# Attention scores as float32 products of two heads on the two row halves of the array, instead of float32r parts of one head

## The chip, the core and the metric

The kernel runs on one core of a Trainium2 chip. The metric is device time in microseconds of one execution; the median of three runs is given. The core has five engines with queues of their own: PE (TensorE, matmuls; PEld is its weight load), DVE (VectorE), ACT (ScalarE), POOL (GpSimd) and SP, which here issues the DMAs. Each engine takes its instructions in order, and an instruction waits for semaphores that other engines raise. SBUF is the working memory of 128 partitions, PSUM the accumulators that PE writes: 8 banks of 512 float32 columns. POOL can't read PSUM.

## The reference

Causal attention with a decay from forget gates, for 8 batches and 8 heads of 576 positions and 64 dimensions; its output is the input of a feed-forward part with a gate.

```python
def _attn_ref(q, k, v, f):
    scores = scale * np.matmul(q, k.transpose(0, 1, 3, 2))        # scale = 1 / sqrt(64)
    cum = np.cumsum(np.log(np.clip(f, 0.0001, 1.0)), axis=-1)
    scores = np.where(causal, -1e9, scores + cum[:, :, :, None] - cum[:, :, None, :])
    attn = np.exp(scores - np.max(scores, axis=-1, keepdims=True))
    attn = attn / (np.sum(attn, axis=-1, keepdims=True) + 1e-09)
    return np.matmul(attn, v)

def _moe_ref(x, w_in, w_out):          # 4608 x 512, 512 x 2048, 2048 x 512
    h = x @ w_in
    return (h * erf(softplus(h))) @ w_out
```

## The kernel before, in words

The attention is one loop over steps `t`, one head of the 64 (batch times heads) per step, pipelined over six steps. The feed-forward part follows; its first four steps are mixed into the last steps of the loop.

**A head.** Its 576 queries are cut into blocks `i` = 0 to 4 of 64, 128, 128, 128 and 128 rows; block `i` needs the keys up to `END[i]` = 64, 192, 320, 448, 576, so causality saves the rest. Block 0 (the corner) sits on partitions 64 to 127. The scores of a head have 64 + 192 + 320 + 448 + 576 = 1600 columns.

**Scores.** `load` fetches `qr` and `kr` with the 64 dimensions twice, on both halves of the 128 partitions, and `c`, the decay sums of the head, broadcast to all partitions. `prep` splits them into float32r parts: `kh` (DVE) is `kr` rounded, `kl` (POOL, L346) is the rest; `qs` holds rounded `q` on the upper half (DVE, L353) and the rest of `q` on the lower (DVE, L354). A product over 128 rows with `kh` and one with `kl` make the full product. `scores` puts blocks into four banks of the pool `ps_s`, adds the causal mask on the diagonal blocks by a product with `eye` and `upper` (L374), and DVE reduces each (L380): it adds `c`, writes the result to `pr` in SBUF and keeps the row minimum in `st` (signs are turned, so this is the maximum). Block 4 is spread over two banks and takes two reductions.

**After the scores.** In step t+1 ACT takes the exponentials of the five blocks in place (`exps`, L410), with row sums into `st`. In `normalize` DVE adds 1e-9 (L416), takes the reciprocal (L417), and POOL multiplies the five blocks (L421). In step t+3 (`LAG`) PE transposes the head in two halves: banks t0 and t1, then t2 and t3 (L439; the 64-row corners into t3, L452). ACT copies the banks to `pt` (L459, L460, L462, L463). The pool of these banks has two buffers, so t2 and t3 wait for copies of earlier ones. Between the halves of the transposes PE multiplies by the values (L476, pairs of heads on the two column halves of the array; group 0 or 1 of a pair, by turns), and `store` copies the result `o` to `xo` (DVE for group 0, ACT for group 1, L496), which is stored to `xt_d`.

Into each step from t = 4 on, a piece of `convert` is mixed, which prepares the weights of the feed-forward part: in a cycle of four steps a load, one ACT and one DVE operation, two DVE operations, two DVE and one POOL operation (L280 to L297).

**What sets the order.** PE and ACT keep the order in which the code emits (`ORDERED`). For DVE, POOL and SP a scheduler places the instructions when the kernel is built; the order is then fixed. Which of the two buffers a transpose bank gets is also settled then.

The names of `Moe` (feed-forward): `up` makes `ph` (L117), `gate` makes `gh` and `gl`, `down` makes `y`; `RINGS` says how many buffers `e`, `gh` and `gl` have.

Of the kernel before, what the change touches and what calls it, by code (L numbers as in the profile page):

```python
# [11 lines left out]
F32 = mybir.dt.float32  # L12
# [23 lines left out]


# [9 lines left out]
LAG = 3  # L47
EARLY = 2
# [9 lines left out]
class Moe:  # L58
# [6 lines left out]
    RINGS = {"e": 10, "gh": 4, "gl": 5}  # L65
# [151 lines left out]
def attention_moe(ctx, tc, q2, k2, vp, f, w_in, w_out, out):  # L217
# [85 lines left out]
    with ExitStack() as ph:  # L303
# [3 lines left out]
        ps_s = early.enter_context(tc.tile_pool(name="ps_s", bufs=4, space=PSUM, side="right"))  # L307
# [12 lines left out]
        heads, vals = {}, {}  # L320

        def load(n):
            b, h = divmod(n, H)
            qr = io.tile([P, 64 + S], F32, name=f"qr{n}", tag="qr")
            nc.sync.dma_start(out=qr, in_=q2[b, h])
            kr = io.tile([P, S], F32, name=f"kr{n}", tag="kr")
            nc.sync.dma_start(out=kr, in_=k2[b, h])
            c = io.tile([P, S], F32, name=f"c{n}", tag="c")
            if n:
                nc.sync.dma_start(out=c, in_=cum_d[n:n + 1].rearrange("a s -> (a s)").partition_broadcast(P))  # L330
            heads[n] = [qr, kr, c]
# [6 lines left out]
        def prep(n, step):  # L338
            if step == 0:
                qr, kr, c = heads[n]  # L340
                qs = io.tile([P, 64 + S], F32R, name=f"qs{n}", tag="qs")
                kh, kl = (io.tile([P, S], F32R, name=f"{nm}{n}", tag=nm) for nm in ("kh", "kl"))
                cm = io.tile([P, 64], F32, name=f"cm{n}", tag="cm")
                heads[n] = [qs, kh, kl, c, cm, qr]
                nc.vector.tensor_copy(out=kh, in_=kr)
                nc.gpsimd.tensor_tensor(out=kl, in0=kr, in1=kh.bitcast(F32), op=ALU.subtract)  # L346
            elif step == 1:
                c, cm = heads[n][3:5]
                nc.gpsimd.affine_select(out=cm[64:], in_=c[64:, :64], pattern=[[-1, 64]], compare_op=ALU.is_ge,  # L349
                                        fill=MASK, base=0, channel_multiplier=1)  # L350
            else:
                qs, qr = heads[n][0], heads[n].pop()
                nc.vector.tensor_copy(out=qs, in_=qr)  # L353
                nc.vector.tensor_tensor(out=qs[64:, 64:], in0=qr[64:, 64:], in1=qs[64:, 64:].bitcast(F32),  # L354
                                        op=ALU.subtract)
# [251 lines left out]
```

## Time and profile before

| | |
|---|---|
| median of three runs | 1250.14 us (1249.97 to 1251.14) |
| the profiled execution | 1250.38 us, span of the profile 1248.2 us |
| busy, share of the span | PE 1184.1 us (95%), PEld 1021.8 (82%), ACT 673.5 (54%), POOL 651.0 (52%), DVE 620.1 (50%) |
| DMA | 130.22 MB, mean 104 GB/s |
| granted TensorE clock | 0.999 |

The page gives busy times over the whole span, which mixes two stages: up to about 415 us the attention, from 440 us the feed-forward part. So the views below are taken for stretches of time. In a list of groups a row has the line, engine, operation and tile, the count, busy time and mean, then the engine's idle time before it and what ended it. In a timeline a row has start and duration; `x7` means seven instructions merged. A matmul of float32 operands leaves two records, a transpose one.

### The profile page before, as it was taken

How to read it: one execution, taken by the hardware profiler on the slowest of the kernel's cores; microseconds unless marked ns; L12 is line 12 of the kernel's file. 1: busy time of each engine (PE TensorE's matmuls, PEld its weight loads, DVE VectorE, ACT ScalarE, POOL GpSimd, SP SyncE). 2: the span in 40 equal slices, each digit the busy share in tenths (PEclk: the TensorE clock that was granted, in tenths of full speed). 3: DMA queues.
4: the chain of work that ended last, by engine and by line, in shares of the span. 5: the costliest groups of instructions: out<-in, count | busy, mean ns of one | idle time of the engine just before them, and what ended most of it. 6: DMA issues, size and time to landing. Idle time of an engine off the chain costs nothing.

```text
span 1248.2 us, 22854 instructions
## 1 busy us (share of the span) xinstructions
PE 1184.1 (95%) x8576; PEld 1021.8 (82%) x8576; DVE 620.1 (50%) x1630; ACT 673.5 (54%) x1392; POOL 651.0 (52%) x723
## 2 busy tenths in 40 slices
PE   5888889898898999999999999999999999999998
PEld 4666667676676799999999999999999999999987
DVE  8999998999999346565431221321212212212121
ACT  4888777877787867666542332423423324224332
POOL 4999999999999535444343332322322323313221
PEclk9999999999999999999999999999999999999999
DMA  7767676676664313233122131111101101101000
GB/s 218 248 188 245 219 227 203 203 238 215 223 195 157 117 61 118 69 104 99 51 85 68 51 100 54 59 61 34 35 1 35 35 1 35 34 1 34 18 17 18
DMA packets 65838, 130.22 MB, mean 104 GB/s; under 512 B 5696, under 2 KB 20032, under 8 KB 65728
## 3 DMA queue, kind: packets, MB, share of 16 engines
q1 hardware_dynamic: 65728, 128.77, 32.3%
q8 instruction: 67, 1.10, 0.3%
q14 instruction: 43, 0.35, 0.1%
HBM read 105.01 MB, written 23.74 MB: 103 GB/s over the span
## 4 chain that ended last, share of the span: by engine, by line
PE 74%; POOL 14%; issue 7%; ACT 2%; DVE 2%; DMA 1%; POOLq 0%; SPq 0%; ACTq 0%
PE ph L117 33%; POOL pr L421 13%; PE y L156 11%; PE y L154 11%; PE y L155 11%; PE o L476 5%; PE t L439 3%; ACT pr L410 1%; POOL cm L349 1%; POOL kl L346 1%; ACT pt L462 1%; DVE pr L380 0%; DMA xt_d<-xo 0%; ACT xo L496 0%; DVE qs L354 0%
## 5 line engine op out<-in xcount | busy, mean ns | idle before, releaser
L117 PE MATMUL ph<-xh,w 128*128 128x256 f32 x2304 | 436.2, 283 | 0.0
L117 PEld LDWEIGHTS ph<-xh,w 128*128 128x128 f32 x2304 | 367.3, 191 | 6.0
L135 POOL TENSOR_TENSOR gl<-e,gh 128x512 fp32r<-128x512 f32 x144 | 189.0, 1322 | 317.8 <-DVE gh L134 316.1
L123 ACT ACTIVATE e<-ph 128x512 f32<-128x512 f32 x144 | 86.1, 598 | 458.7 <-PE ph L117 458.1
L117 PE MATMUL ph<-xl,w 128*128 128x256 f32 x1152 | 325.5, 283 | 0.0
L421 POOL TENSOR_SCALAR pr<-pr,st 128x192 f32<-128x192 f32 (+4 forms) x320 | 242.3, 766 | 12.8 <-ACT pt L459 0.7
L156 PE MATMUL y<-w,gl 128*128 128x512 f32 x576 | 228.5, 397 | 0.0
L154 PE MATMUL y<-w,gh 128*128 128x512 f32 x576 | 228.3, 396 | 0.0
L155 PE MATMUL y<-w,gh 128*128 128x512 f32 x576 | 227.3, 395 | 0.0
L117 PEld LDWEIGHTS ph<-xl,w 128*128 128x128 f32 x1152 | 219.5, 191 | 5.7
L410 ACT ACTIVATE pr<-pr,st 128x576 f32<-128x576 f32 (+4 forms) x320 | 177.4, 556 | 17.8 <-DVE st L380 14.4
L134 DVE CAST gh<-e 128x512 fp32r<-128x512 f32 x144 | 62.5, 452 | 206.1 <-PE y L155 200.3
L132 DVE TENSOR_TENSOR e<-e,ph 128x512 f32<-128x512 f32 x144 | 92.7, 683 | 115.0 <-ACT e L126 113.6
L439 PE MATMUL t<-ident,pr 128*128 128x128 f32 x640 | 107.3, 287 | 43.7 <-POOL pr L421 40.7
L103 POOL TENSOR_TENSOR xl<-xr,xh 128x1024 fp32r<-128x1024 f32 x27 | 65.0, 2408 | 155.7 <-ACT xh L102 155.7
L156 PEld LDWEIGHTS y<-w,gl 128*128 128x128 f32 x576 | 108.8, 189 | 25.8
L155 PEld LDWEIGHTS y<-w,gh 128*128 128x128 f32 x576 | 108.9, 189 | 20.7
L154 PEld LDWEIGHTS y<-w,gh 128*128 128x128 f32 x576 | 108.9, 189 | 19.6
L380 DVE CUSTOM_DVE_ANT_0 pr<-s,c 128x288 f32<-128x288 f32 (+3 forms) x256 | 112.8, 477 | 21.0 <-PE s L369 18.9
L439 PEld LDWEIGHTS t<-ident,pr 128*128 128x128 f32 x640 | 68.9, 140 | 57.0 <-POOL pr L421 48.9
L476 PE MATMUL o<-pt,v 64*64 64x64 f32 (+2 forms) x1408 | 112.9, 299 | 0.0
L476 PEld LDWEIGHTS o<-pt,v 128*64 128x64 f32 (+1 forms) x1408 | 73.8, 136 | 41.0 <-issue 21.0
(62 smaller groups left out, 1437.7 us busy)
## 6 DMA issues: line engine op xcount, KB each, us to landing
qr<-in_q_dram SPq DMA_DIRECT2D x64, 320.0 KB, 4.5
kr<-in_k_dram SPq DMA_DIRECT2D x64, 288.0 KB, 3.3
c<-cum_d SPq DMA_DIRECT2D x63, 288.0 KB, 5.3
xr<-xt_d SPq DMA_DIRECT2D x27, 512.0 KB, 4.1
v<-in_vp_dram SPq DMA_DIRECT2D x32, 320.0 KB, 5.4
xt_d<-xo SPq DMA_DIRECT2D x32, 288.0 KB, 5.6
wraw<-in_w_in_dram SPq DMA_DIRECT2D x16, 512.0 KB, 4.8
wraw<-in_w_out_dram SPq DMA_DIRECT2D x16, 512.0 KB, 4.3
```

Source lines behind the costliest of these rows:

```text
L117: nc.tensor.matmul(out=ps[:, e], lhsT=w[:, kd, fs], rhs=x[:, kd], start=kd == 0 and n == 0, stop=kd == KD - 1 and n == 2)
L123: self.nc.scalar.activation(out=e_, in_=self.ps[j], func=AF.Softplus)
L132: nc.vector.tensor_mul(e_, e_, h_)
L135: nc.gpsimd.tensor_tensor(out=gl, in0=e_, in1=gh.bitcast(F32), op=ALU.subtract)
L154: nc.tensor.matmul(out=y[tb], lhsT=gh[:, cs], rhs=wh[:, e], start=first, stop=False)
L155: nc.tensor.matmul(out=y[tb], lhsT=gh[:, cs], rhs=wl[:, e], start=False, stop=False)
L156: nc.tensor.matmul(out=y[tb], lhsT=gl[:, cs], rhs=wh[:, e], start=False, stop=last)
L380: nc.vector.tensor_tensor_reduce(out=pr[r, TOFF[i] + k0:TOFF[i] + k1], in0=s[bank][r, at:at + k1 - k0], in1=(c if i else cm)[r, k0:k1], sc ...
L410: nc.scalar.activation(out=seg, in_=seg, func=AF.Exp, bias=m[r, i:i + 1], scale=-1.0, accum_out=l[r, i:i + 1])
L421: nc.gpsimd.tensor_scalar(out=seg, in0=seg, scalar1=rl[r, i:i + 1], scalar2=1.0, op0=ALU.mult, op1=ALU.mult)
L439: nc.tensor.transpose(out=t[:, at:at + P], in_=pr[:, TOFF[i] + ch * P:TOFF[i] + ch * P + P], identity=ident)
L476: nc.tensor.matmul(out=o[64 * j:64 * j + 64, a - q0:b - q0], lhsT=v[:rows, ch, 64 * j:64 * j + 64], rhs=pts[2 * p + j][:rows, at:at + b - ...
```

## The change

The unit is now a pair of heads: two steps, `half` 0 (blocks 4 and 1 of both heads) and `half` 1 (blocks 3, 2 and the corner of both).

- `q` and `k` come from memory once per pair: the first head's 64 dimensions on partitions 0 to 63, the second's on 64 to 127. There are no float32r parts: `prep`, `kh`, `kl` and `qs` are gone.
- Each block is a float32 product over 64 rows, of one head on the upper row half of the array and of the other on the lower. The two write to score tiles of their own, of two banks each (`ps_s` has two such tiles instead of four single banks). `PARTS` says which block goes where, and block 4's two parts now lie in one tile, so that it is reduced by one operation over 576 columns.
- Corner masks, memsets, the addition of 1e-9 and the reciprocal are done for both heads at once; there are two additions and two reciprocals for a pair, for half 0 (`128x4`) and half 1 (`128x6`).
- `LAG` is 4 instead of 3, `pr` has 6 buffers instead of 4, and there is no early normalization of the first heads.
- The copies of bank t1 and of group 1 of `o` go from ACT to DVE. Rings of the feed-forward part: `e` 9 instead of 10, `gl` 4 instead of 5.

On DVE, the end of a head's reductions and what follows, before (head 40 is being reduced; `st39` are the sums of the head before it, whose exponentials ACT runs in this step; rows of `128x1` and `64x1` read out a minimum):

```order
L380 ISA pr40_3999,st40_4000<-s3_40_4005,c40_3682 128x320 [waits PE_49]
L380 ISA st40_4000 128x1
L380 ISA pr40_3999,st40_4000<-s3_40_4005,cm40_3794 64x64 [waits Pool_49]
L380 ISA st40_4000 64x1
L416 TENSOR_SCALAR st39_3900<-st39_3900 128x5 [waits Activation_49]
L345 CAST kh43_4090<-kr43_3977 128x576 [waits DMAHW6_49]
L417 RECIPROCAL st39_3900<-st39_3900 128x5 [waits DVE_49]
L353 CAST qs43_4089<-qr43_3975 128x640 [waits DMAHW7_49]
L354 TENSOR_TENSOR qs43_4089<-qr43_3975,qs43_4089 64x576 [waits DVE_49]
```

On DVE now, from the end of step 20 (half 0 of pair 10) into step 21 (half 1 of it):

```order
L446 COPY pt16_1547<-t1_16_1553 128x512 [waits PE_49]
L482 COPY xo7_1571<-o7_0_1560 128x320 [waits DMAHW4_49,PE_49]
L398 TENSOR_SCALAR st9_1209<-st9_1209 128x6 [waits Activation_49]
L399 RECIPROCAL st9_1209<-st9_1209 128x6 [waits DVE_49]
L398 TENSOR_SCALAR st10_1365<-st10_1365 128x4 [waits Activation_49]
L377 ISA pr20_1525,st10_1365<-s10_1_0_1594,c10_1194 128x448 [waits PE_49]
L377 ISA st10_1365 128x1
L377 ISA pr20_1525,st10_1365<-s10_1_0_1594,c10_1194 128x320
L377 ISA st10_1365 128x1
L377 ISA pr20_1525,st10_1365<-s10_1_0_1594,cm10_1361 64x64
```

Before, the addition for exponentials of the running step stood behind the step's reductions. Now the addition `128x4` for half 0 of pair 10, whose exponentials ACT runs in step 21, stands ahead of the reductions of step 21. The addition `128x6` stands behind the reductions of its step.

On PE, the end of the values and the second half of the transposes, before (every step alike):

```order
L476 MATMUL o17_1_4048<-pt34_3736,v17_3583 64x64
L476 MATMUL o17_1_4048<-pt35_3836,v17_3583 64x64
L439 MATMUL t2_37_4063<-ident_63,pr37_3700 128x128 [waits Activation_49]
L439 MATMUL t2_37_4063<-ident_63,pr37_3700 128x128
L452 MATMUL t3_37_4066<-ident_63,pr37_3700 64x64 [waits Activation_49]
L452 MATMUL t3_37_4066<-ident_63,pr37_3700 64x64 x4
L369 MATMUL s0_41_4101<-kh41_3891,qs41_3890 128x288 [waits DVE_49]
```

On PE now, in the even step 20 and then in the odd step 21:

```order
L425 MATMUL t2_16_1573<-ident_63,pr16_1213 128x128 [waits Activation_49]
L425 MATMUL t2_16_1573<-ident_63,pr16_1213 128x128
L438 MATMUL t3_16_1576<-ident_63,pr16_1213 64x64 [waits Activation_49,Pool_49]
L438 MATMUL t3_16_1576<-ident_63,pr16_1213 64x64 x4
L366 MATMUL s10_1_0_1594<-k10_1191,q10_1190 64x64 [waits DVE_49]
```
```order
L425 MATMUL t2_17_1644<-ident_63,pr17_1214 128x128 [waits Activation_49]
L425 MATMUL t2_17_1644<-ident_63,pr17_1214 128x128
L438 MATMUL t3_17_1647<-ident_63,pr17_1214 64x64 [waits DVE_49,Pool_49]
L438 MATMUL t3_17_1647<-ident_63,pr17_1214 64x64 x4
L366 MATMUL s11_0_0_1679<-k11_1347,q11_1346 128x320 [waits DMAHW1_49,DMAHW0_49]
```

Before, t3 waits for ACT's copy of t1 (L460) in every step. Now the wait differs by step: in even steps t2 waits for ACT's copy of t0 and t3 for ACT's copy of t2, of the same step; in odd steps t2 waits for ACT's copy of t0, and t3 for DVE's copy of t1.

The diff, cut to its core:

```diff
+PARTS = [[(192, 4, 0, 320), (512, 4, 320, 576), (0, 1, 0, 192)], [(448, 0, 0, 64), (0, 3, 0, 448), (512, 2, 0, 320)]]
+REDUCED = [[(192, 4), (0, 1)], [(0, 3), (512, 2), (448, 0)]]
+PLACE = {4: 0, 1: 1, 0: 2, 3: 3, 2: 4}
...
-LAG = 3
-EARLY = 2
+LAG = 4
...
-    RINGS = {"e": 10, "gh": 4, "gl": 5}
+    RINGS = {"e": 9, "gh": 4, "gl": 4}
...
-        ps_s = early.enter_context(tc.tile_pool(name="ps_s", bufs=4, space=PSUM, side="right"))
+        ps_s = early.enter_context(tc.tile_pool(name="ps_s", bufs=2, space=PSUM, side="right"))
...
+        def load(p):
+            q, k = (io.tile([P, S], F32, name=f"{nm}{p}", tag=nm) for nm in ("q", "k"))
+            nc.sync.dma_start(out=q, in_=q2[p // NP, p % NP])
+            nc.sync.dma_start(out=k, in_=k2[p // NP, p % NP])
+            c = io.tile([P, 2, S], F32, name=f"c{p}", tag="c")
+            if p:
+                for j in range(2):
+                    n = 2 * p + j
+                    nc.sync.dma_start(out=c[:, j], in_=cum_d[n:n + 1].rearrange("a s -> (a s)").partition_broadcast(P))
+            pairs[p] = [q, k, c]
...
+        def corner_mask(p):
+            c = pairs[p][2]
+            cm = io.tile([P, 2, 64], F32, name=f"cm{p}", tag="cm")
+            nc.gpsimd.affine_select(out=cm[64:], in_=c[64:, :, :64], pattern=[[0, 2], [-1, 64]],
+                                    compare_op=ALU.is_ge, fill=MASK, base=0, channel_multiplier=1)
+            st = wk.tile([P, 3, 2 * NB], F32, name=f"st{p}", tag="st", bufs=4)
+            nc.gpsimd.memset(st[:64, 1, 4:6], 1.0)
...
+        def scores(p, half):
+            q, k, c, cm, st = pairs[p]
+            s = [ps_s.tile([P, 1024], F32, name=f"s{p}_{half}_{j}", tag="s") for j in range(2)]
...
+            for at, i, k0, k1 in PARTS[half]:
+                for j in range(2):
+                    h = slice(64 * j, 64 * j + 64)
+                    nc.tensor.matmul(out=s[j][ROWS[i], at:at + k1 - k0], lhsT=q[h, START[i] if i else 0:END[i]],
+                                     rhs=k[h, k0:k1], start=True, stop=i == 0 or k1 < END[i])
+            for at, i, k0, k1 in PARTS[half]:
+                if i and k1 == END[i]:
+                    for j in range(2):
+                        nc.tensor.matmul(out=s[j][:, at + START[i] - k0:at + k1 - k0], lhsT=eye, rhs=upper,
+                                         start=False, stop=True)
+            for j in range(2):
+                pr = probs[2 * p + j]
+                for at, i in REDUCED[half]:
+                    r, m = ROWS[i], 2 * PLACE[i] + j
+                    nc.vector.tensor_tensor_reduce(
+                        out=pr[r, TOFF[i]:TOFF[i] + END[i]], in0=s[j][r, at:at + END[i]],
+                        in1=(c if i else cm)[r, j, :END[i]], scale=-0.125, scalar=BIG, op0=ALU.add, op1=ALU.min,
+                        accum_out=st[r, 0, m:m + 1])
...
+        def normalize(p, half):
+            st = stats[p]
+            at = slice(4, 10) if half else slice(0, 4)
+            l, rl = st[:, 1, at], st[:, 2, at]
             nc.vector.tensor_scalar(out=l, in0=l, scalar1=1e-9, scalar2=None, op0=ALU.add)
             nc.vector.reciprocal(out=rl, in_=l)
+            for j in range(2):
...
             if half == 0:
                 nc.scalar.copy(out=pt[:, 0:512], in_=banks[0])
-                nc.scalar.copy(out=pt[:, 512:1024], in_=banks[1])
+                nc.vector.tensor_copy(out=pt[:, 512:1024], in_=banks[1])
...
-            (nc.scalar.copy if g else nc.vector.tensor_copy)(out=xo[:, q0:q1], in_=held.pop((p, g))[:, :q1 - q0])
+            nc.vector.tensor_copy(out=xo[:, q0:q1], in_=held.pop((p, g))[:, :q1 - q0])
...
+            p, half = divmod(t, 2)
+            if half == 0 and t + 4 < NHD:
+                load(p + 2)
...
+            if 0 <= t - 2 < NHD:
+                normalize(*divmod(t - 2, 2))
...
+            if half == 0 and t + 2 < NHD:
+                corner_mask(p + 1)
             if new:
-                scores(t)
+                scores(p, half)
             if old:
-                exps(t - 1, (4, 1, 0, 3, 2))
...
+                exps(*divmod(t - 1, 2))
```

More of the change, by code (lines that the diff above doesn't have):

```diff
@@ L336, in load_values @@
             vals[p] = v
[L338 to L355, printed above, removed]
@@ L424, in attention_moe @@
+            if half:
+                del stats[p]
         pts = {}
```

140 lines of the change are left out of this document (39 added, 101 removed).

## The prediction

> **What bounds the kernel now.** I read the page first, then the stages, the waits, and at last one step of the attention instruction by instruction.
>
> ```profile
> 50.00:400.00 350.00, 311.93 (x2942) 241.44 (x2943) 323.62 (x1035) 281.08 (x817) 328.21 (x457) 1.00 0.68 215
> 440.00:1248.00 808.00, 803.72 (x5081) 725.83 (x5079) 237.51 (x418) 333.50 (x432) 267.49 (x183) 1.00 0.15 49
> ```
>
> The columns are busy time (count) of PE, PEld, DVE, ACT and POOL, then clock, DMA share and GB/s. From 440 us on TensorE is full, and the change touches nothing there but two ring sizes (9 instead of 10 buffers `e`, 4 instead of 5 `gl`). From 50 to 400 us POOL (94%), DVE (92%) and PE (89%) are all nearly full; DMA is not. Everything is decided in this stage.
>
> ```profile
> PE t L439 <- POOL pr L421: 38.1, 39, 1.6
> L421 POOL TENSOR_SCALAR pr<-pr,st 128x192 f32<-128x192 f32 x278 | 217.0, 789 | 10.4
> L346 POOL TENSOR_TENSOR kl<-kr,kh 128x576 fp32r<-128x576 f32 x55 | 77.8, 1414 | 3.4
> ```
>
> The longest wait of PE is the transposes' for POOL's normalization. So POOL sets today's pace, and it spends 1.41 us per head on `kl`, which the change removes.
>
> ```profile
> L463 ACT COPY pt<-t x64: 418/420/423, 32.1 to 429.4; 64x320 f32<-64x320 f32 x64
> 410.71 0.47 PE L452 MATMUL t<-ident,pr 64*64 64x64 f32 x5
> ```
>
> Copies of bank t3 run from 32.1 to 429.4 us: 63 intervals of 6.31 us. The last step with scores (t = 63) has its t3 at 410.7 us.
>
> The step itself (start and duration first); then one pair of the values' records; then a DVE instruction beside one of POOL, and ACT's release of t3; then three groups with their means:
>
> ```profile
> 207.69 1.37 PE L476 MATMUL o<-pt,v 128*64 128x256 f32 x20
> 208.98 0.44 PE L439 MATMUL t<-ident,pr 128*128 128x128 f32 x2
> 209.35 0.47 PE L452 MATMUL t<-ident,pr 64*64 64x64 f32 x5
> 209.46 0.37 ACT L462 COPY pt<-t 128x256 f32<-128x256 f32 x1 [0.97 <-PE t L439]
> 209.75 0.40 PE L369 MATMUL s<-kh,qs 128*128 128x288 f32 x1
> 209.86 0.42 ACT L463 COPY pt<-t 64x320 f32<-64x320 f32 x1
> 210.18 0.78 ACT L410 ACTIVATE pr<-pr,st 128x576 f32<-128x576 f32 x1
> 210.72 0.40 PE L374 MATMUL s<-upper,eye 128*128 128x128 bf16 x4
> 210.95 0.44 ACT L410 ACTIVATE pr<-pr,st 128x192 f32<-128x192 f32 x1
> 211.51 0.34 ACT L410 ACTIVATE pr<-pr,st 64x64 f32<-64x64 f32 x1
> 211.74 0.33 PE L439 MATMUL t<-ident,pr 128*128 128x128 f32 x1
> 211.78 0.35 DVE L380 CUSTOM_DVE_ANT_0 pr<-s,c 128x192 f32<-128x192 f32 x1
> 211.97 0.67 ACT L410 ACTIVATE pr<-pr,st 128x448 f32<-128x448 f32 x1
> 212.37 0.98 PE L439 MATMUL t<-ident,pr 128*128 128x128 f32 x7 [0.30 <-POOL pr L421]
> 212.49 0.62 DVE L380 CUSTOM_DVE_ANT_0 pr<-s,c 128x448 f32<-128x448 f32 x1
> 212.64 0.55 ACT L410 ACTIVATE pr<-pr,st 128x320 f32<-128x320 f32 x1
> 213.04 0.49 DVE L380 CUSTOM_DVE_ANT_0 pr<-s,c 128x320 f32<-128x320 f32 x1
> 213.19 0.56 ACT L459 COPY pt<-t 128x512 f32<-128x512 f32 x1
> 213.28 2.11 PE L476 MATMUL o<-pt,v 128*64 128x256 f32 x24
> 213.56 0.23 DVE L380 CUSTOM_DVE_ANT_0 pr<-s,cm 64x64 f32<-64x64 f32 x1
> 213.83 0.32 DVE L416 TENSOR_SCALAR st<-st 128x5 f32<-128x5 f32 x1
> 215.32 0.44 PE L439 MATMUL t<-ident,pr 128*128 128x128 f32 x2
> ```
> ```profile
> 213.76 0.39 PE L476 MATMUL o<-pt,v 128*64 128x256 f32 x2
> ```
> ```profile
> 219.62 1.41 POOL L346 TENSOR_TENSOR kl<-kr,kh 128x576 fp32r<-128x576 f32 x1
> 219.99 0.58 ACT L460 COPY pt<-t 128x512 f32<-128x512 f32 x1
> 220.17 0.88 DVE L416 TENSOR_SCALAR st<-st 128x5 f32<-128x5 f32 x1
> 220.76 0.35 PE L452 MATMUL t<-ident,pr 64*64 64x64 f32 x3
> ```
> ```profile
> L280 ACT ACTIVATE wtop<-wraw 128x512 f32<-128x512 f32 x14 | 9.5, 675 | 0.0
> L416 DVE TENSOR_SCALAR st<-st 128x5 f32<-128x5 f32 x56 | 26.0, 464 | 1.3
> L185 DVE COPY yo<-y 128x512 f32<-128x512 f32 x34 | 23.5, 691 | 112.9 <-PE y L156 112.9
> ```
>
> **The change part by part.**
>
> *PE, scores.* Today 209.75 to 211.74: 1.99 us a head. A float32 product costs more passes, but the values show the price, since theirs are float32 too, on two column halves. Their records come in pairs (at 213.76 two, 0.39 us for both together), and 20 records for 384 full-height and 192 corner columns per head take 208.98 − 207.69 = 1.29 us, 24 records for 896 and 128 take 2.04. The difference, 0.75 us for 448 columns, is 1.67 ns a column for both heads together. The new scores have 768 columns per head in an even step, 832 in an odd one: 1.28 and 1.39 us if the row halves overlap as the column halves do. With four masks (the 0.40 us row, less its pipeline tail of 0.2) and 0.2 and 0.35 for one and two more changes of tile shape (the values' 1.29 us leave 0.33 beside 576 × 1.67 ns for their own two) I get 1.7 and 1.95 us: about what is removed. If they do not overlap, 1.28 and 1.39 more; that is the upper end, and a gain beyond this I exclude, as no pass is dropped. Lower end and value taken: overlap, the nearest row being the same float32 product on two halves.
>
> *POOL.* 1.41 us per head less; masks and memsets merge. *DVE.* Three casts and a subtraction of `qs`, `kh` go, two reductions merge into one of 576; two PSUM copies come. *DMA* carries less, at a share of 0.68 now. On SP the second half of a pair's `c` now stands behind the store of an earlier pair's `xo`, but loads run four steps ahead. None of this earns or costs anything unless the pace comes from there, so I put it at nothing and follow what each engine waits for in the new order.
>
> *The wait that is added.* DVE now has the `1e-9` addition of a pair's first half in front of the reductions of its second half, and that addition waits for four exponentials which ACT runs in that same odd step. Queued behind it are six reductions and then the copy of bank t1, which has moved from ACT to DVE; in an odd step PE's t3 waits for this copy, and behind t3 stand all the scores of the next step. Before, the addition stood behind the reductions. So an odd step is one chain, from t3 to t3:
> - t3 to the copy of t3: 209.86 − 209.35 = 0.51; to the first exponential 0.32.
> - exponentials of 576, 192, 576, 192: 0.77 + 0.56 + 0.77 (start to start), the last 0.44 with 0.08 to read its sum: 2.62. Now at 3.45. To DVE 0.05 (bounds 0 and the 0.19 that ACT to PE takes with a weight load: 220.76 − 220.57).
> - the addition: 0.46 by its mean, 0.07 overlapped as in the other DVE rows (0.62 busy, 0.55 to the next): 0.39. Bounds 0.1 and 0.9.
> - six reductions: 448, 320 and 64 take 0.55 + 0.52 + 0.27, twice: 2.68.
> - the 128x512 copy out of PSUM 0.69; to t3 0.19.
>
> Sum: 3.45 + 0.05 + 0.39 + 2.68 + 0.69 + 0.19 = 7.45 us. PE alone would need 0.40 + 1.95 + 1.03 + 2.04 + 0.37 = 5.8 (score start after t3, scores, eight transposes, values, t2; seven transposes take 213.28 − 212.37 = 0.91, an eighth 0.11 more).
>
> An even step has no such addition in front: its reductions (192 columns 0.35 − 0.07; 576 by the 1.0 ns a column between the 320 and 448 rows 0.68; twice) and copy end at 0.40 + 1.8 + 1.92 + 0.69 = 4.8 us. But t2 there waits for ACT's copy of t0, behind six exponentials, and t3 for the copy of t2: 0.83 + 2 × (0.67 + 0.55 + 0.46) + 0.56 + 0.19 gives t2 at 4.94; its copy starts 0.48 later (209.46 − 208.98) and takes 0.37; 0.19 more: 5.98 us. In every second even step ACT first does the weights' absolute value, 0.675 less 0.1 overlap: 6.55. PE alone: 0.40 + 1.7 + 1.03 + 1.29 + 0.37 = 4.8.
>
> Four steps: 2 × 7.45 + 5.98 + 6.55 = 27.4 us, 6.86 a step against 6.31. POOL's work falls to some 4.5 us a step, so the cover of its removed work is this chain. Where a stall goes: PE's wait for POOL becomes a wait for DVE's copy of t1.
>
> The `L416` row at 220.17 ends at 221.05, just when the POOL instruction of 219.62 ends (221.03). The Trainium skill (SBUF — State Buffer, "SBUF: two separate sides") says that DVE in a two-port mode and POOL lock each other out for a whole instruction; by that alone the addition would take about 0.15 plus half a normalization, an estimate of 0.55, and the sum below would be 3 us more. The trace agrees in that row; I keep the mean.
>
> *The sum.* Transposes start in step 4 instead of 3, but the steps ahead of it are short (no transposes), so I leave the first t3 where it is, at 31.6 (bounds ±4: three scans instead of two, but no casts in front). Then 59 intervals of 6.86 reach step 63 at 436.3 us, 25.6 later than 410.7. One head more is left for PE after it: transposes 1.03, values 1.67 on average, 0.77 for t2 and t3: 3.5. The first intervals, in which ACT is not yet behind, give back some 2. So +27 us on the profiled execution, whose 1250.4 us (span 1248.2) is 0.2 above the median: **1277 us**. The feed-forward part keeps its length: an `e` lives four of its steps and a `gl` two, below 9 and 4.
>
> **Rivals.**
> - *Relief passes through (faster).* POOL is the bound, its bound falls, and PE is next: 4.8 + 0.3 and 5.8, about 5.46 a step, gives 31.6 + 59 × 5.46 + 3.5 = 357 against 411: 1197 us. For it: POOL's 94% and the wait rows. Against: it needs the addition's wait to be over before the scores are; it decides below 6.37 a step, so odd steps would have to fall from 7.45 to 6.45. The Trainium skill (Perfetto Trace Analysis, "Identifying the Most-Contended Engine") would say this: optimize the engine of highest occupancy. No run yet tells.
> - *Row halves do not overlap.* Even steps: t2 waits for PE at 0.40 + 2.98 + 1.03 + 1.29 = 5.70, t3 at 6.74. Odd steps: scores end at 3.7, still before the addition, so nothing. 28.4 for four, 7.1 a step: 1291 us. For it: no row-half pair is in the trace. Against: the column pairs. The Trainium skill (TensorE: Matmul & The Clock Gate, Part 3) reports overlap of row tiles, 3.07 times for four, which would make this rival unlikely.
> - *The chain is shorter than its parts* (additions at 0.15, copies released sooner): near 6.4 a step, 1250 us.
>
> **How the numbers follow.** Forecast 0.79, no overlap 0.12, relief 0.05, short chain 0.04. The addition's bounds alone move the time by −8 and +15 us, the start by ±4; the range 1261 to 1295 holds the forecast with these and the no-overlap case. 0.2% (2.5 us) is about what a measurement of this kernel can tell. Faster 0.06 (relief, part of the short chain), same 0.03, slower 0.91.
>
> **What would show it.** Right: copies of t3 spaced in turn about 7.4 and 6.0 to 6.5 us; POOL near 70% from 50 to 400 us; DVE waiting over 1 us for ACT at the addition in odd steps; PE's largest wait for DVE's copy of t1. Score pairs a few ns apart show the overlap. Wrong: odd steps below 6.5 us, or score records one after the other.

## The result, and the profile after

The changed kernel takes 1284.76 us (median of 4 runs, 1284.12 to 1285.54), the kernel before 1250.06 us in the same job: 1.0276 times as long, interval 1.0258 to 1.0294. The forecast was 1277 us, with a range of 1261 to 1295. The profiled execution took 1285.29 us, its span is 1283.5 us.

The two stages, in the columns of the prediction's first fence (busy PE, PEld, DVE, ACT, POOL, then clock, DMA share, GB/s), and the copies of t3 (now at L449):

```profile
50.00:400.00 350.00, 283.52 (x2728) 199.17 (x2727) 223.61 (x781) 224.28 (x675) 166.17 (x321) 0.96 0.48 153
440.00:1283.00 843.00, 837.46 (x5410) 752.86 (x5408) 254.51 (x451) 355.33 (x472) 280.40 (x203) 1.00 0.16 51
```
```profile
L449 ACT COPY pt<-t x64: 418/418/421, 39.3 to 468.5; 64x320 f32<-64x320 f32 x64
```

The feed-forward part is as full of PE as before, and no longer: from the last copy of t3 to the end of the span are 815.0 us, against 818.8 before. In the attention every engine has become idler: POOL fell from 94% to 47%, DVE from 92% to 64%, ACT from 80% to 64%, and PE from 89% to 81%, part of it at a lower clock (0.96). Nobody is the bound; they wait for each other. The first t3 copy comes at 39.3 us instead of 32.1, and the step has grown: from the first to the 60th copy an interval is 6.85 us on average, against 6.33 before by the same count.

The waits between 50 and 400 us (total us, times, longest):

```profile
DVE st L398 <- ACT pr L391: 78.7, 26, 4.0
...
PE t L438 <- DVE pt L446: 27.0, 21, 1.4
PE t L425 <- ACT pt L445: 24.9, 25, 1.3
...
PE t L438 <- ACT pt L448: 13.3, 24, 0.6
```

PE no longer waits for POOL. DVE waits 3.0 us (78.7 / 26) in every odd step for ACT at the addition, and PE waits for the copy of t1 behind it. An odd step of the timeline, from t3 to t3, with the instructions between left out:

```profile
203.27 0.44 PE L438 MATMUL t<-ident,pr 64*64 64x64 f32 x5 [0.55 <-ACT pt L448]
203.74 0.42 ACT L449 COPY pt<-t 64x320 f32<-64x320 f32 x1 [0.62 <-PE t L438]
204.19 0.78 ACT L391 ACTIVATE pr<-pr,st 128x576 f32<-128x576 f32 x1
...
206.72 0.17 DVE L398 TENSOR_SCALAR st<-st 128x4 f32<-128x4 f32 x1 [3.96 <-ACT pr L391]
206.80 0.62 DVE L377 CUSTOM_DVE_ANT_0 pr<-s,c 128x448 f32<-128x448 f32 x1
...
209.48 0.69 DVE L446 COPY pt<-t 128x512 f32<-128x512 f32 x1
...
210.31 0.33 PE L438 MATMUL t<-ident,pr 64*64 64x64 f32 x3 [1.24 <-DVE pt L446]
210.44 0.50 PE L366 MATMUL s<-k,q 64*128 64x320 f32 x1
210.48 0.27 PE L438 MATMUL t<-ident,pr 64*64 64x64 f32 x2
```

This is the predicted chain: ACT's four exponentials, the addition, six reductions, the copy of t1, t3: 210.31 − 203.27 = 7.04 us. The following even step ends with ACT's copy of t0, t2, the copy of t2, t3:

```profile
215.27 0.58 ACT L445 COPY pt<-t 128x512 f32<-128x512 f32 x1
...
215.91 0.44 PE L425 MATMUL t<-ident,pr 128*128 128x128 f32 x2 [1.30 <-ACT pt L445]
...
216.38 0.37 ACT L448 COPY pt<-t 128x256 f32<-128x256 f32 x1 [0.53 <-PE t L425]
...
216.90 0.44 PE L438 MATMUL t<-ident,pr 64*64 64x64 f32 x5 [0.55 <-ACT pt L448]
```

It takes 216.90 − 210.31 = 6.59 us. The intervals between copies repeat 7.05, 6.58, 7.09, 6.01; but once in twelve steps one is 8.4 us, and the clock says why. Slices of 2 us around such a place, then the first 40 us of the changed kernel, then 20 to 40 us of the kernel before (the clock is the third figure from the end):

```profile
106.00:108.00 2.00, 1.45 (x12) 1.11 (x13) 2.00 (x8) 0.97 (x3) 0.16 (x1) 0.56 0.87 278
108.00:110.00 2.00, 2.00 (x8) 0.86 (x6) 0.19 (x2) 2.00 (x7) 1.76 (x2) 0.50 0.62 226
110.00:112.00 2.00, 2.00 (x13) 1.47 (x10) 1.22 (x4) 0.32 (x2) 1.81 (x5) 0.50 0.24 40
112.00:114.00 2.00, 2.00 (x15) 1.31 (x15) 1.87 (x11) 0.58 (x1) 0.69 (x3) 0.73 0.75 275
114.00:116.00 2.00, 2.00 (x27) 1.48 (x25) 1.06 (x3) 0.55 (x2) 0.11 (x1) 1.00 0.40 143
```
```profile
0.00:20.00 20.00, 8.21 (x34) 4.71 (x34) 10.74 (x30) 7.19 (x17) 2.72 (x15) 1.00 0.76 229
20.00:40.00 20.00, 15.86 (x70) 10.09 (x71) 8.80 (x39) 9.78 (x32) 10.95 (x25) 0.57 0.46 168
```
```profile
20.00:40.00 20.00, 16.59 (x100) 13.06 (x99) 19.07 (x66) 15.80 (x49) 16.01 (x24) 1.00 0.87 257
```

TensorE falls to half its clock for about 6.8 us (1.8 + 2 + 2 + 1.1 by the first four slices), behind the stall at the end of an even step, at 106, 188, 270, 352 and 434 us; and it stays there from 21 to 38 us, through most of the first transposes (ten take 2.31 us at 35.92, eight 1.04 us at 41.14). The 1.00 of the kernel before is not full speed throughout: four records of its 128x192 scores take 1.65 us at 23.32 and 0.76 us at 32.38, so it too was slow until about 26 us. None of this was in the prediction.

### The profile page after: what moved, and what is told of

It is laid out like the page before. It is cut to its first block, busy times and chain, and to the rows that moved or that the text cites. A ratio compares the mean times of both kernels' runs of the same rounds, so it can differ in the third digit from the quotient of the medians.

```text
span 1283.5 us, 22120 instructions
## 1 busy us (share of the span) xinstructions
PE 1185.0 (92%) x8576; PEld 995.1 (78%) x8576; DVE 531.7 (41%) x1409; ACT 631.8 (49%) x1297; POOL 483.2 (38%) x595
## 4 chain that ended last, share of the span: by engine, by line
PE 65%; ACT 1%; DVE 0%; issue 0%; POOL 0%; POOLq 0%
PE ph L122 32%; PE y L161 11%; PE y L159 10%; PE y L160 10%; PE o L462 1%; ACT pr L391 1%; PE t L425 0%; PE s L366 0%; DVE pr L377 0%; PE t L438 0%; ACT pt L445 0%; ACT pt L449 0%; DVE pt L446 0%; ACT L285 0%; ACT wtop L285 0%
## 5 line engine op out<-in xcount | busy, mean ns | idle before, releaser
L405 POOL TENSOR_SCALAR pr<-pr,st 128x576 f32<-128x576 f32 (+3 forms) x320 | 175.7, 562 | 116.8 <-PE t L438 67.2
L391 ACT ACTIVATE pr<-pr,st 128x576 f32<-128x576 f32 (+3 forms) x320 | 176.6, 553 | 16.7 <-DVE st L377 13.5
L377 DVE CUSTOM_DVE_ANT_0 pr<-s,c 128x576 f32<-128x576 f32 (+3 forms) x256 | 129.6, 552 | 38.6 <-POOL pr L405 25.4
L366 PE MATMUL s<-k,q 64*128 64x320 f32 (+4 forms) x768 | 130.9, 449 | 15.5 <-DMA k<-in_k_dram 8.5
L425 PE MATMUL t<-ident,pr 128*128 128x128 f32 x640 | 100.9, 292 | 28.9 <-ACT pt L445 28.8
L366 PEld LDWEIGHTS s<-k,q 64*128 64x128 f32 (+1 forms) x768 | 81.3, 197 | 40.4 <-issue 25.1
```

Of the source, the lines that this page charges most:

```text
L366: nc.tensor.matmul(out=s[j][ROWS[i], at:at + k1 - k0], lhsT=q[h, START[i] if i else 0:END[i]], rhs=k[h, k0:k1], start=True, stop=i == 0 or ...
L377: nc.vector.tensor_tensor_reduce(out=pr[r, TOFF[i]:TOFF[i] + END[i]], in0=s[j][r, at:at + END[i]], in1=(c if i else cm)[r, j, :END[i]], sc ...
L391: nc.scalar.activation(out=seg, in_=seg, func=AF.Exp, bias=st[r, 0, m:m + 1], scale=-1.0, accum_out=st[r, 1, m:m + 1])
L405: nc.gpsimd.tensor_scalar(out=seg, in0=seg, scalar1=st[r, 2, m:m + 1], scalar2=1.0, op0=ALU.mult, op1=ALU.mult)
L425: nc.tensor.transpose(out=t[:, at:at + P], in_=pr[:, TOFF[i] + ch * P:TOFF[i] + ch * P + P], identity=ident)
```

## Experiments

Each kernel is told by its difference from the changed kernel or from another of the table; the times are medians, the ratio is to the kernel before in the same job.

| kernel | us | ratio, interval |
|---|---|---|
| changed kernel | 1284.76 | 1.0276, 1.0258 to 1.0294 |
| A: DVE in code order | 1283.42 | 1.0256, 1.0241 to 1.0272 |
| B: t1's copy on ACT | 1231.32 | 0.9844, 0.9829 to 0.9858 |
| C: exponentials split in even steps | 1260.47 | 1.0071, 1.0056 to 1.0086 |
| D: A, B and C together | 1189.53 | 0.9503, 0.9487 to 0.9519 |
| E: A with fillers on PE | 1254.83 | 1.0037, 1.0025 to 1.0049 |
| F: changed kernel with fillers, also at the start | 1277.81 | 1.0220, 1.0199 to 1.0241 |
| G: D with scores head after head | 1260.25 | 1.0074, 1.0050 to 1.0099 |
| H: kernel before without `kl` | 1206.25 | 0.9643, 0.9628 to 0.9657 |
| I: D with products at the start | 1185.36 | 0.9471, 0.9457 to 0.9485 |
| J: D with DVE's order left to the scheduler (B and C) | 1225.19 | 0.9805, 0.9764 to 0.9846 |
| K: D with the addition in front again | 1220.67 | 0.9753, 0.9737 to 0.9770 |
| L: D with t1's copy on DVE | 1207.25 | 0.9650, 0.9635 to 0.9664 |

My theory was that the addition's wait, with t1's copy behind it on DVE, and ACT's chain in even steps set the pace. Rivals: the scores cost more on PE than they seem to; the copies were moved to the wrong engine, or ACT is the bound; later, the clock.

**A: DVE in code order.**

```diff
-ORDERED = {mybir.EngineType.Activation, mybir.EngineType.PE}
+ORDERED = {mybir.EngineType.Activation, mybir.EngineType.PE, mybir.EngineType.DVE}
```

> The changed kernel with DVE kept in code order, so that the addition of half 0 stands behind the reductions of half 1 and the copy of t1, not in front of them. Theory (the added wait): in odd steps the reductions start when the masks are done, 2.5 us after t3, end 2.68 later, and t1's copy with the way to t3 adds 0.83: 6.0 us instead of 7.05. Even steps keep their 6.0 and 6.6, since ACT's six exponentials set those. Four steps 24.6 us, 6.15 a step: 59 times 0.54 us off the 6.69 of the undisturbed steps, 32 us less, 1253 us, or 1243 if the half-clock stretches of 6.5 us go as well (about 10 us in all). Rival 1 (the cost of the scores on PE, by row halves that run one after the other): PE's work is the same, so within 5 us of 1285. Rival 2 (the exchange between the copies on DVE and ACT): odd steps would stay near 7, since t1's copy is still on DVE; within 10 us of 1285.

Measured: 1283.42 us. By the time alone, the theory had fallen. The trace says otherwise: DVE no longer waits at the addition, and PE no longer for t1's copy, yet nearly every odd step takes 7.33 to 7.39 us. PE there, and the clock's fall in two windows of 3.4 us (columns as above):

```profile
210.83 1.37 PE L462 MATMUL o<-pt,v 128*64 128x256 f32 x20
213.49 0.44 PE L425 MATMUL t<-ident,pr 128*128 128x128 f32 x2 [1.29 <-ACT pt L445]
214.48 0.44 PE L438 MATMUL t<-ident,pr 64*64 64x64 f32 x5 [0.55 <-ACT pt L448]
214.85 2.53 PE L366 MATMUL s<-k,q 64*64 64x64 f32 x12
```
```profile
212.40:215.80 3.40, 1.76 (x15) 1.20 (x17) 2.27 (x6) 2.20 (x6) 1.62 (x5) 1.00 0.00 0
215.80:219.20 3.40, 3.40 (x17) 2.23 (x14) 1.28 (x7) 2.43 (x9) 2.17 (x6) 0.50 0.26 55
```

A window in which PE is busy for 1.76 us of 3.4 is followed by one at half clock, and the scores behind the stall, which run into it, take 2.53 us. The two steps are 7.35 + 6.3 = 13.65 us, four such windows, and the falls come 13.65 us apart: the same stall meets the same place in nearly every pair of steps. The mean granted clock from 50 to 400 us is 0.88. At two steps, where the clock stayed up, the copies stand 6.02, 6.57, 6.02, 6.01 us apart: the 6.0 that the theory expects. E tests this.

**E: A with fillers.** The fillers' results are not used. In E and F the buffers of the transposes are written into the code as they stood without fillers.

```diff
+                if half == 0:
+                    fill(held[p - 3, 0], 384, 3)   # three products ident x ident into o's free columns
                 store(*divmod(t - LAG - 2, 2))
```

> The kernel with DVE in code order, and in each even step three float32 products of 128 columns (about 0.2 us each) that nothing uses, into free columns of o's bank, placed on PE between the values and t2, where it waits 0.7 to 1.3 us for ACT's copy of t0. The banks of the transposes are written out as they stood without them. Theory (the clock took the gain back): without the fillers the odd steps fall to 6.02 us where the clock is full, as at two places of that run, but nearly everywhere TensorE runs at half clock for 3.4 us behind the even step's stall, and they take 7.35. With less idle time the clock stays up: odd steps 6.0, even 6.0 to 6.6, mean 6.15 to 6.2 instead of 6.79, 35 to 38 us less than 1283: 1246 to 1250. Rival 1 (another wait holds the odd steps at 7.35, and the lower clock only accompanies it): 1283 or, with the fillers' time on the path, up to 20 us more. Rival 2 (PE's work itself is the price): slower by the fillers, 1290 to 1303.

Measured: 1254.83 us, 28.6 less than A, by adding work to PE. The same place, with the fillers at L457:

```profile
207.80 1.37 PE L467 MATMUL o<-pt,v 128*64 128x256 f32 x20
209.10 0.94 PE L457 MATMUL o<-ident 128*128 128x128 f32 x6
209.89 0.44 PE L426 MATMUL t<-ident,pr 128*128 128x128 f32 x2
210.88 0.44 PE L439 MATMUL t<-ident,pr 64*64 64x64 f32 x5 [0.55 <-ACT pt L449]
211.25 1.82 PE L366 MATMUL s<-k,q 64*64 64x64 f32 x12
```

The scores take 1.82 us again, the mean clock from 50 to 400 us is 0.99, and the intervals are 6.02, 6.57, 6.02, 6.01 nearly throughout; three of 7.4 to 7.6 us, and 9.4 and 7.3 near the end, are left where the clock still fell, and the time ends 5 us above the range. E is 29.9 us below the changed kernel: the edit to DVE's order, with the clock kept up, is worth about that, and in A the clock took it back. The rivals "another wait" and "PE's work" fall.

**B: t1's copy on ACT; C: exponentials split around the copy of t0.**

```diff
-                nc.vector.tensor_copy(out=pt[:, 512:1024], in_=banks[1])
+                nc.scalar.copy(out=pt[:, 512:1024], in_=banks[1])
```
```diff
-                exps(*divmod(t - 1, 2))
+                exps(*divmod(t - 1, 2), (0,) if half == 0 else (0, 1))
             if out_:
                 transposes(t - LAG, 0)
                 evacuate(t - LAG, 0)
+            if old and half == 0:
+                exps(*divmod(t - 1, 2), (1,))
```

> The changed kernel with one line changed: the copy of bank t1 back on ACT. The addition stays in front of the reductions. Theory: the wait costs only because t1's copy, and so PE's t3, stands behind it on DVE. With the copy on ACT, t3 is free 0.83 + 2.62 + 0.56 + 0.58 + 0.19 = 4.8 us after the one before, and PE's own 5.8 us bind in odd steps; in even steps t3 waits for t1's copy, which follows t0's directly, instead of t2's: about 0.5 us earlier, 5.5 and 6.0. Four steps 23.1, 5.8 a step: 1285 minus 59 times 0.9 = 53 us gives 1232, and 1222 if the half-clock stretches go too. Rival 1 (PE's scores): no change beyond 5 us. Rival 3 (ACT is the bound, so work must not go back to it): slower, 0.58 us more in each of 64 steps, 1310 to 1320.

> The changed kernel with ACT's order in even steps altered: exponentials of the first head, copy of t0, exponentials of the second head. The addition's wait stays. Theory: in even steps t0 is ready on PE at 2.9 us after t3 and its copy ends at 3.4, so t2 waits for PE only; t3 comes at 5.2 to 5.7 us instead of 6.0 and 6.6. Odd steps keep 7.05. Four steps about 25.1, 6.27 a step: 59 times 0.42 = 25 us less, 1260, and a few us less if the half-clock stretches, which begin at the even steps' stall of PE, go as well. Rival 1 (PE's scores): within 5 us of 1285. Rival: only DVE's wait counts and gives the even step's time back in the odd one: within 10 us of 1285.

Measured: 1231.32 and 1260.47 us, each as expected. In B the intervals are mostly 5.77 and 5.95 in odd steps, 5.6 and 6.2 in even ones; DVE still waits at the addition (83.3 us in 35 waits from 50 to 400 us), but t3 no longer stands behind it. ACT takes back 0.58 us a step and the kernel gains 53 us: ACT was not the bound. In C the even steps are 4.94 and 6.08, the odd ones 7.05 to 7.8.

**D: all three.**

> All three edits: DVE in code order, t1's copy on ACT, ACT's exponentials of even steps split around the copy of t0. Theory: nothing but PE is left, which needs 5.7 us in odd and 4.9 in even steps by its own rows, 5.3 a step: 59 times 1.39 = 82 us less than the undisturbed 6.69, 1203 us, 10 less if the half-clock stretches go; faster than before (1250) and near the 1197 of the rival in which the relief passes through. If the row halves did not overlap, PE would need 1.3 us more per step and the time could not fall below about 1270.

Measured: 1189.53 us, 5% faster than before and 3.5 below the lower of the two times expected. PE is the bound now:

```profile
50.00:400.00 350.00, 347.99 (x3471) 256.56 (x3470) 235.22 (x855) 315.66 (x879) 202.52 (x375) 1.00 0.56 174
```

PE is busy for 348 of 350 us at full clock; the mean interval is 5.22 us. The change is sound; its order was not.

**G: scores head after head, in D.**

```diff
-            for at, i, k0, k1 in PARTS[half]:
-                for j in range(2):
+            for j in range(2):
+                for at, i, k0, k1 in PARTS[half]:
```

> The kernel with all three edits (1189.5 us), with the scores emitted head after head instead of head beside head: all products of the first head, on the upper row half, then all of the second, on the lower. The same instructions otherwise. Theory (row halves overlap when their products alternate): PE is the bound in that kernel, and each step pays what the overlap saved, 1.28 us in even and 1.39 in odd steps by the prediction's price of 1.67 ns a column; 64 steps, 85 us, about 1275. Rival (the halves run one after the other anyway): no change, 1190. Rival (the pieces overlap only in part): between, in proportion.

Measured: 1260.25 us, 70.7 more. The scores of an odd step and of the even step behind it, in D and then in G:

```profile
238.86 1.82 PE L366 MATMUL s<-k,q 64*64 64x64 f32 x12
...
244.35 0.51 PE L366 MATMUL s<-k,q 64*128 64x320 f32 x1
...
244.54 1.51 PE L366 MATMUL s<-k,q 64*128 64x320 f32 x11
```
```profile
250.59 3.55 PE L366 MATMUL s<-k,q 64*64 64x64 f32 x12
...
257.78 0.53 PE L366 MATMUL s<-k,q 64*128 64x320 f32 x1
...
258.15 1.83 PE L366 MATMUL s<-k,q 64*128 64x320 f32 x11
```

So row halves do overlap when their products alternate, and this rival falls. About 3 us of the profiled execution are one fall of the clock (at 186.5 us, an interval of 10.03 us instead of 6.78). The price was uneven: 3.55 − 1.82 = 1.73 us in the odd step instead of 1.39, and 2.20 − 1.70 = 0.50 in the even one (from its first product to the end of its last) instead of 1.28. In the even step the single records show the second head's first product starting beside the first head's second one, ahead of the first head's third: part of the overlap came back by itself. The Trainium skill (TensorE: Matmul & The Clock Gate, Part 3) says that row tiles overlap, and the trace agrees; it also says that matmuls start in strict order, and the rows of the changed kernel at 210.44 and 210.48 differ: a score product, emitted behind all five transposes of t3 and on the other row half, starts before two of them.

**H: the kernel before without POOL's `kl`**, one tile `kl0` for all heads.

```diff
-                kh, kl = (io.tile([P, S], F32R, name=f"{nm}{n}", tag=nm) for nm in ("kh", "kl"))
+                kh, kl = io.tile([P, S], F32R, name=f"kh{n}", tag="kh"), kl0
...
-                nc.gpsimd.tensor_tensor(out=kl, in0=kr, in1=kh.bitcast(F32), op=ALU.subtract)
+                if n == 0:
+                    nc.gpsimd.tensor_tensor(out=kl, in0=kr, in1=kh.bitcast(F32), op=ALU.subtract)
```

> The kernel before, without POOL's subtraction for kl of all heads but the first: every head uses the first one's kl, so this part of the computation is left out. Everything else stands as before. Theory (POOL set the pace before, so its relief is real): POOL falls from 5.9 to 4.5 us a head, and the next bounds are DVE with 5.8 and PE with 5.6: about 5.9 a step instead of 6.31, 24 us less, 1226 (range 1215 to 1240). Rival (POOL was full but not the bound): within 3 us of 1250. The difference between this and the changed kernel's 1285 is then what the added wait costs beside the relief.

Measured: 1206.25 us, 44.6 less; I had expected 24. POOL's share falls to 70% and PE is full:

```profile
50.00:400.00 350.00, 345.23 (x3266) 271.69 (x3263) 315.28 (x1073) 308.66 (x873) 245.31 (x423) 1.00 0.72 223
```

So POOL did set the pace before, and its relief is real: a part of the gain that the change could have passed through. That I fell short is DVE's: I took its 5.8 us a step for work, but part of that were DVE instructions stretched beside POOL's (the cast to `qs`, `L353`, took 0.70 us before and takes 0.48 here).

**K and L: D with one half of the pair put back**, the addition in front of the reductions (K, where `reductions` is the last part of `scores`), or t1's copy on DVE (L, that is A and C without B).

```diff
             if old:
                 exps(*divmod(t - 1, 2), split)
+            if old and half:
+                addition(p, 0)
+            if new and half:
+                reductions(p, half)
```

> The kernel with all three edits (1189.5 us) with the added wait put back alone: on DVE the addition of half 0 stands in front of the reductions of half 1 again, while t1's copy stays on ACT, the weights' conversion stays where code order has it, and the exponentials of even steps stay split. Theory (the wait costs through what stands behind it): no t1 copy is behind it now, but the reductions of half 1 are; they start 3.45 us after t3 as in the changed kernel and end at 6.2, while that kernel's PE asks for the second score tile 5.05 + 0.4 us after t3. So the next step's scores come about 0.75 us later: 24 us over 32 pairs, 1213 (1205 to 1235, the upper end if the clock falls as well). Rival (the wait is free once t1's copy is gone from DVE): 1189 to 1192.

> The kernel with all three edits with the other half put back alone: t1's copy on DVE, the addition behind the reductions. Theory: odd steps are 2.5 + 2.68 + 0.83 = 6.0 us, as measured in the kernel with DVE in code order alone (6.02), even ones 4.94 to 6.09 as with the split exponentials alone; mean 5.77 instead of 5.22, 32 us more, 1222 (1210 to 1235). Together with the run that puts the wait back: if each alone costs much less than both (1260, the run with the split alone), the price is of the two in series on DVE, not of either. Rival (the copy's engine is indifferent): 1189 to 1192.

Measured: 1220.67 us (+31.1), in the range, and 1207.25 us (+17.7), 2.8 below it, since the longer even steps are 5.34 us and not 6.09. Each half costs; so the rival that the copies were moved to the wrong engine holds in part, for t1's copy costs 17.7 us on DVE even with the addition out of its way. (The copy of group 1 of `o` was not moved back.) With both halves back and the split kept there is only C, 1260.47 (+70.9); but C also has the weights' work in a row, which J below prices, and a clock of 0.95 from 50 to 400 us, so whether the two halves cost more together than one by one is not shown. What K pays for, on DVE and PE:

```profile
205.26 0.51 DVE L399 TENSOR_SCALAR st<-st 128x4 f32<-128x4 f32 x1 [2.84 <-ACT pr L394]
...
207.40 0.43 PE L366 MATMUL s<-k,q 64*128 64x320 f32 x1
...
208.08 0.23 DVE L380 CUSTOM_DVE_ANT_0 pr<-s,cm 64x64 f32<-64x64 f32 x1
...
208.37 1.56 PE L366 MATMUL s<-k,q 64*128 64x320 f32 x10 [0.54 <-DVE st L380]
```

The reductions end at 208.3, and the scores of the next step wait for the second score tile. Odd steps are 5.05 us (5.05 and 4.56 by turns in D); the even ones grow from 5.34 and 5.83 to 6.3 to 6.6. The weights' work stands where D has it, so this is the price of the addition's place alone.

**J: D with DVE's order left to the scheduler** (B and C without A).

> The kernel with all three edits less one: DVE's order is the changed kernel's again, so the addition of half 0 stands in front of the reductions of half 1, while t1's copy is on ACT and the exponentials of even steps are split. Theory (the wait costs only through what stands behind it on DVE and PE's t3): t3 is free of it, but the reductions of half 1 still end at 6.2 us of an odd step, so ACT's exponentials of the next step and the scores that reuse the tiles come later than PE could: 0.1 to 0.4 us a step more than 5.22, 1195 to 1215. Rival (once t1's copy is gone from DVE the wait is free): 1189 to 1191.

Measured: 1225.19 us, above the range, but the run does not show what it was made for. The expectation assumed that the scheduler would put the addition in front again. It did not: in this kernel the addition stands behind the six reductions in every pair from 50 to 400 us, as in D. On DVE, the end of an odd step's reductions and the addition:

```profile
204.19 0.23 DVE L377 CUSTOM_DVE_ANT_0 pr<-s,cm 64x64 f32<-64x64 f32 x1
...
204.46 0.17 DVE L398 TENSOR_SCALAR st<-st 128x4 f32<-128x4 f32 x1
```

So J says nothing of the addition. What differs from D on DVE is the place of the weights' work (and of a few copies of `o`). Three of four intervals are those of D (5.34, 5.05, 5.83); the fourth, an odd one, is 5.9 to 6.2 us instead of 4.56, and 7.5 to 7.8 in the seven places where the clock fell as well. In the even step ahead of it four instructions of the weights stand in a row on DVE in front of the reductions, and the odd step's scores wait for their tiles:

```profile
206.54 0.89 DVE L286 SCALAR_TENSOR_TENSOR wtop<-wtop,wraw 128x512 f32<-128x512 f32 x1 [1.25 <-ACT wtop L285]
...
208.78 0.69 DVE L298 SCALAR_TENSOR_TENSOR wtop<-wtop,wraw 128x512 int32<-128x512 int32 x1
...
209.40 0.75 DVE L377 CUSTOM_DVE_ANT_0 pr<-s,c 128x576 f32<-128x576 f32 x1
...
211.44 1.82 PE L366 MATMUL s<-k,q 64*64 64x64 f32 x10 [0.63 <-DVE st L377]
```

So edit A does two things: it moves the addition and spreads the weights' work. K prices the first alone and J the second (35.7 us, the clock's part included), both in the frame of D. In the changed kernel the weights' four stand there too, but its even steps were held by ACT: the odd step behind them takes 7.09 us and the other odd step 7.05, and both take 6.02 in E. So the weights' four cost 0.04 us in four steps there, and what E gains is the end of the addition's wait; whether moving the addition alone, with the four left in a row, would gain as much is not shown.

**F: the changed kernel with fillers in even steps and at the start; I: D with products at the start only.**

```diff
+        warm = ps_o.tile([P, 512], F32, name="warm", tag="o")
+        fill(warm, 0, 12)
...
+            if t < LAG:
+                fill(warm, 0, 5)
+            elif t < LAG + 2:
+                fill(warm, 0, 6)
```

> The changed kernel (addition in front, as predicted on) with the same fillers in even steps, and with products that nothing uses at the start: 12 before the first scores, 5 behind the scores of steps 0 to 3, 6 in steps 4 and 5. Theory: two of the changed kernel's costs are the clock's. The stretches of 6.5 us at half clock every 82 us go: 59 intervals of 6.69 instead of 6.85, 10 us less. And at the start TensorE is fast before the first transposes: t3's first copy at 32 to 35 us instead of 39.3. Together 1285 less 14 to 17: 1268 to 1271. Odd steps stay at 7.05, since the wait is untouched. Rival (the late start is the chain of exponentials, additions and scans, and the 8.4 us intervals a DMA's): no change of either, 1285, or some us more.

> The kernel with all three edits (1189.5 us) and the unused products at the start alone: 12 before the first scores, 5 behind the scores of steps 0 to 3, 6 in steps 4 and 5. Theory: its t3 copies start at 41.3 us because TensorE runs at half clock until 38 us, as in the changed kernel, where the same products brought them from 39.3 to 34.1. Five us less, 1184 to 1185, and no stretch at half clock after 20 us. Rival (in this kernel DVE's order sets the start): no change, 1189 to 1190.

Measured: 1277.81 and 1185.36 us, so 7 and 4.2 us less. In F t3's first copy comes at 34.1 instead of 39.3 us: 5.1 of the 7.2 us by which the changed kernel starts late are the clock's. In the loop the expectation failed: the mean interval is 6.81 instead of 6.85, since half-clock stretches of 3.4 us came at other places: five of the eight between 100 and 400 us still start at an even step's t3 (155, 210, 237, 264 and 292 us), in spite of the fillers there, and three behind the odd step's wait for t1's copy (176, 312 and 381 us). I is the fastest kernel of the study, 5.3% below before.

## Why the prediction was right, and where it was not

- *The added wait as the pace-setter, direction and place: right.* DVE waits 3.0 us at the addition in odd steps, PE's largest wait is the one for t1's copy, and B, K and E show that what stands behind the addition is what costs.
- *The odd step, 7.45 us: 0.40 too long.* Measured 7.04. The terms as the rows give them: t3 to its copy 0.47, to the first exponential 0.45, exponentials 2.50 (taken 2.62), to DVE 0.03, the addition 0.08 start to start (taken 0.39), reductions 2.68, t1's copy with the way to t3 0.83 (taken 0.88). The addition was the mis-sized term. I took the mean of L416 where POOL ran beside it; in the changed kernel POOL has finished by then. The rule on the shared ports that I weighed (0.55; the Trainium skill, SBUF — State Buffer, "SBUF: two separate sides") would have been further off here; but in K, where POOL multiplies from 203.45 to 206.68, the addition takes 0.51 and ends at 205.77, as one of these multiplications does (205.75), which is what that rule would have.
- *The even step, 5.98 and 6.55: right* (6.01 and 6.58), by ACT's chain as worked out, and C confirms that chain.
- *6.86 us a step: right by two errors.* Without lowered clock four steps are 7.05 + 6.58 + 7.09 + 6.01 = 26.73, 6.68 each. The half-clock stretches add the rest, 0.17 each or 10 us, to 6.85.
- *The first t3 at 31.6, bounds ±4: failed.* Its copy came 7.2 us later than before; I looked at DVE's scans and casts and not at TensorE's clock, at which the first scores run. This step carries the miss: 7.2 for the start, 2 for the first intervals that gave nothing back, less 0.5 for the intervals and 0.5 for the tail are 8.2 us; 1277 + 8.2 = 1285.2, and the profiled execution took 1285.3.
- *The price of the scores, 1.67 ns a column for two heads: right.* From the first score product to the first transpose behind the masks are 1.83 us in even steps and 1.99 in odd ones, against 1.7 and 1.95, and in G the alternation is worth 70.7 us. The sign named for overlap, pairs a few ns apart, came in odd steps (217.523 and 217.530 us); in even steps the records start 0.13 to 0.19 us apart.
- *POOL near 70%: wrong*, 47%. I kept the normalizations' 0.79 us; the same blocks now take 0.56 (140.0 us for 256 in the list of groups), beside a DVE that is idle more; that this is the cause is argued, not shown. It cost nothing in time, for POOL had slack.
- *Relief passes through:* its premise is shown by H, its end by D (1189.5 against my 1197). The Trainium skill (Perfetto Trace Analysis, "Identifying the Most-Contended Engine") would start with the busiest engine; in the kernel before the runs agree with it. In the changed kernel every engine is below 82%, and there the order decides.

## What to carry to other kernels

Where a unit of work is split into halves, look at each instruction that waits for the half now running on another engine, and at everything queued behind it on its own engine: here one small addition in front of reductions and a copy, with ACT's order, turned a relief of POOL that is worth 44.6 us (H) into a loss of 35. Undo such waits together as well as one at a time: A alone gained nothing, and the three edits gained 95 us. When a removed wait brings no time, look at the granted clock before dropping the theory. And where a scheduler places instructions, read the order in the trace of each variant before reading its time: J was built to put the addition in front and did not.

## What the runs showed of the hardware

- TensorE's clock halves for 3.4 or about 6.8 us behind stretches in which PE waits. In the 3.4 us before such a fall PE was busy for 1.6 to 2.2 us in A, 2.4 in E and 1.9 to 2.4 in F, with single gaps no longer than 1.5 us. That is no threshold: J has windows with 2.4 us busy that a fall followed (at 141 us) and others that none followed (at 213 us), and in G the clock fell once, at 186.5 us, though PE was busy throughout the 3.4 us before. A loop whose stall meets such a window every time can hold itself there: A ran at 0.88 of the clock from 50 to 400 us. The Trainium skill (TensorE: Matmul & The Clock Gate, Part 1) tells of two clock states and a free-running window of 3.4 us, and the rows agree; its table of states ties the fall to an idle window, and here half a window of work did not prevent it. Why some stretches last one window and others two, and what brought the fall in G, stays open.
- Work that nobody uses, put on PE where it waits, made a kernel 28.6 us faster (E against A), and at the start 4.2 us (I against D).
- In the first 17 us of the changed kernel the clock column shows 1.00, though the twelve records of the first score products, at 8.49 us, take 2.93 us and those of the same shapes 1.66 us from 210.44: before the first recorded change the column doesn't tell the clock.
- PE starts a product on one row half (210.44 us) ahead of transposes that were emitted before it on the other (210.48 us).
